# Three attention heads instead of two per exponential in a fused attention and feed-forward kernel

## The chip, the cores and the metric

One core of a Trainium2 chip runs the whole program. The metric is the device time of one execution in microseconds (us). The profile of an execution counts from its first to its last instruction and is about 1.8 us shorter than that time.

## The reference, cut to what matters

```python
# x is 1 x 2048 x 640 bf16; 32 query heads of 20 columns, one key head, one value head; F = 1536
xn  = layernorm(x)
q   = (xn @ wq) split in 32 heads;  k = xn @ wk;  v = xn @ wv
p   = softmax(q k^T / sqrt(20))          # 32 x 2048 x 2048 exponentials
att = concat(p v) @ wo
ffn = relu(xn @ w1 + b1)**2 @ w2 + b2
out = x + att + ffn
```

The exponentials are the bulk: 32 x 2048 x 2048 numbers, on 128 lanes 1,048,576 columns.

## The kernel before

Queries are taken in 4 chunks of 512 (`QC`), heads in 8 groups of 4 (`G`), keys in 16 tiles of 128 (`KT`). A *block* is one chunk and one group, a *step* is one key tile of a block. In a step TensorE computes the transposed scores of four heads (one bank of PSUM each, the memory `ps` of eight banks of 512 float32 columns that the matmuls write to; the four matmuls side by side on four row strips), ScalarE takes two heads per ACTIVATE, and TensorE multiplies the exponentials with v (P·V) one step behind. The six score banks form a ring of three pairs. The two other banks are the P·V accumulator (`PVB`) and one spare bank (`MB`) for everything else: query projections (QT), the first feed-forward product (FFN), output projections (OUT). Those *units* are cut into groups of four 32-column matmuls that fill the steps. Filler matmuls with zero weights use up what remains, to keep TensorE's clock up.

```python
for j in range(NSTEP):                                  # 512 steps
    b, t = divmod(j, KT)
    for i in range(4):                                  # scores of four heads
        n = 2 * j + i // 2; p = n % 3
        ...   # i == 0 waits for the exponential 2j-2
        matmul(ps[:, 2 * p + i % 2, :], kT[32*i:32*i+DH, tile t], qT[32*i:32*i+DH, ...])
    for a in range(2):                                  # two exponentials of two heads each
        n = 2 * j + a; p = n % 3
        activation(out=PT[:, n % NSLOT, :, :], in_=ps[:, 2*p:2*p+2, :], func=Exp, ...)   # 128x1024
    # (cut) choose the groups of other work and the number of fillers from a time budget
    if j >= 1:
        emit_pv(j - 1, nfill)     # waits for both exponentials of step j-1; at t == 0 also for the
                                  # transpose that empties the accumulator; at t == KT-1 emits
                                  # transpose, reciprocal, multiply, transpose on VectorE
    # (cut) the groups of the unit in hand
```

The softmax here doesn't subtract the row's maximum and nothing guards it: scores larger than these inputs give would overflow.

## Time and profile before

| | us |
|---|---|
| time, median of 15 runs | 977.7 (977.0 to 978.7) |
| profile: prologue, to the start of the first exponential | 25.77 |
| profile: loop, first exponential's start to last one's end | 940.77 |
| profile: tail, to the last instruction | 9.10 |

The profile page of the kernel before: the span, busy times (us, share of the span, instructions), the granted TensorE clock (the share of its full clock that TensorE was allowed) in tenths over 40 slices, the chain that ended last by engine, and its two costliest groups (busy us, mean ns of one, idle time before them and what ended it):

```profile
span 975.6 us, 28817 instructions
...
PE 831.6 (85%) x13373; PEld 316.5 (32%) x13375; DVE 178.8 (18%) x321; ACT 961.6 (99%) x1072; POOL 62.4 (6%) x69
...
PEclk9999999999999999999999999999999999999998
...
ACT 98%; PE 1%; DMA 0%; DVE 0%; ACTq 0%; issue 0%; SPq 0%; DVEq 0%
...
L852 ACT ACTIVATE PT<-ps 128x1024 bf16<-128x1024 f32 x1024 | 940.7, 1107 | 0.6 <-PE ps L843 0.5
L781 PE MATMUL ps<-kT,zeros 128*32 128x512 bf16 x4720 | 315.5, 382 | 0.0
```

ScalarE is the bound, by its exponentials. The chain in order of time (start us, us, what):

```profile
38.78 547.43 ACT PT L852 x596
586.23 379.39 ACT PT L852 x413
```

### The profile page before, as it was taken

The numbers are of one execution on the slowest core, as the hardware profiler recorded it, in microseconds if no ns is written. First come the engines' busy times: TensorE is split into PE (matmuls) and PEld (weight loads), VectorE is DVE, ScalarE is ACT, GpSimd is POOL, SyncE is SP. The second block draws the span as 40 slices with busy tenths as digits, with TensorE's granted clock in tenths as the row PEclk, the third lists the DMA queues.
The fourth block names the chain that finished last, engine by engine and source line by source line (L and its number), as shares of the span: only waits on it lengthen the run. The fifth ranks groups of instructions, "written<-read, shape, count | busy, mean of one in ns | idle before, by whom it ended". The sixth has DMA issues, their size and how long they took to land.

```text
span 975.6 us, 28817 instructions
## 1 busy us (share of the span) xinstructions
PE 831.6 (85%) x13373; PEld 316.5 (32%) x13375; DVE 178.8 (18%) x321; ACT 961.6 (99%) x1072; POOL 62.4 (6%) x69
## 2 busy tenths in 40 slices
PE   7888888888888888888888888888888888888886
PEld 3323223222233333333333333333333333333332
DVE  7221100111111211101111111211202221201123
ACT  8999999999999999999999999999999999999996
POOL 3110000000000000000000000000001001100000
PEclk9999999999999999999999999999999999999998
DMA  9100000000000000000000000000000000000000
GB/s 306 36 1 2 2 2 1 2 2 1 2 2 9 2 8 2 2 8 2 9 2 1 9 2 9 2 9 2 2 9 2 8 2 2 8 2 9 2 9 28
DMA packets 9432, 12.70 MB, mean 13 GB/s; under 512 B 1761, under 2 KB 8674, under 8 KB 9314
## 3 DMA queue, kind: packets, MB, share of 16 engines
q1 hardware_dynamic: 8002, 10.82, 3.4%
q8 instruction: 105, 1.72, 0.7%
q10 hardware_dynamic: 1312, 0.05, 0.1%
q14 instruction: 13, 0.11, 0.0%
HBM read 8.25 MB, written 2.62 MB: 11 GB/s over the span
## 4 chain that ended last, share of the span: by engine, by line
ACT 98%; PE 1%; DMA 0%; DVE 0%; ACTq 0%; issue 0%; SPq 0%; DVEq 0%
ACT PT L852 96%; DMA x_sb<-in_A_x_dram 0%; ACT PT L434 0%; ACT OTn L434 0%; PE ps L221 0%; ACT PT L429 0%; ACT xnT L476 0%; ACT OTn L429 0%; DVE out_sb L357 0%; PE ps L497 0%; PE ps L407 0%; ACTq L84 0%; PE ps L815 0%; ACT vtmp L439 0%; PE ps L843 0%
## 5 line engine op out<-in xcount | busy, mean ns | idle before, releaser
L852 ACT ACTIVATE PT<-ps 128x1024 bf16<-128x1024 f32 x1024 | 940.7, 1107 | 0.6 <-PE ps L843 0.5
L781 PE MATMUL ps<-kT,zeros 128*32 128x512 bf16 x4720 | 315.5, 382 | 0.0
L815 PE MATMUL ps<-PT,vx 128*32 128x512 bf16 x2048 | 201.5, 384 | 74.4 <-ACT PT L852 74.1
L843 PE MATMUL ps<-qT,kT 20*128 20x512 bf16 x2048 | 201.9, 384 | 55.8 <-ACT PT L852 53.3
L781 PEld LDWEIGHTS ps<-kT,zeros 128*32 128x32 bf16 x4720 | 97.9, 95 | 127.9 <-issue 68.7
L843 PEld LDWEIGHTS ps<-qT,kT 20*128 20x128 bf16 x2048 | 51.4, 91 | 269.1 <-ACT PT L852 259.5
L815 PEld LDWEIGHTS ps<-PT,vx 128*32 128x32 bf16 x2048 | 53.7, 95 | 177.2 <-ACT PT L852 148.3
L790 DVE STREAM_TRANSPOSE Tn<-ps 128x512 f32<-128x512 f32 x32 | 23.0, 717 | 416.4 <-PE ps L815 416.4
L269 POOL TENSOR_TENSOR big<-hT_tmp 128x512 bf16<-128x512 bf16 x48 | 49.9, 1040 | 761.0 <-DVE hT_tmp L264 761.0
L221 PE MATMUL ps<-xnT,w_sb 128*32 128x512 bf16 x960 | 68.7, 380 | 0.0
L221 PE MATMUL ps<-w_sb,big 128*32 128x320 bf16 x1536 | 63.6, 300 | 0.0
L264 DVE TENSOR_SCALAR hT_tmp<-ps,b1col 128x512 bf16<-128x512 f32 x48 | 36.0, 750 | 144.0 <-PE ps L221 144.0
L221 PE MATMUL ps<-wo_pad,OTn 128*32 128x320 bf16 x1024 | 47.1, 304 | 2.6 <-DVE OTn L798 2.6
L221 PEld LDWEIGHTS ps<-w_sb,big 128*32 128x32 bf16 x1536 | 40.6, 96 | 15.7 <-issue 6.4
L221 PE MATMUL ps<-xnT,wq_sb 128*20 128x512 bf16 x640 | 45.5, 379 | 0.0
L320 DVE TENSOR_TENSOR out_sb<-ps,x_sb 128x320 bf16<-128x320 f32 x24 | 11.8, 492 | 149.1 <-PE ps L221 149.1
L221 PEld LDWEIGHTS ps<-wo_pad,OTn 128*32 128x32 bf16 x1024 | 27.9, 98 | 14.1 <-DVE OTn L798 2.9
L221 PEld LDWEIGHTS ps<-xnT,w_sb 128*32 128x32 bf16 x960 | 24.1, 96 | 19.5 <-issue 1.7
L246 DVE CAST qT<-ps 128x512 bf16<-128x512 f32 x32 | 22.1, 691 | 10.4 <-PE ps L221 10.4
L798 DVE STREAM_TRANSPOSE OTn<-T 128x512 bf16<-128x512 bf16 x32 | 22.8, 711 | 1.1
L792 DVE TENSOR_TENSOR T<-Tn 128x512 bf16<-128x512 f32 x32 | 22.2, 692 | 1.1
L221 PEld LDWEIGHTS ps<-xnT,wq_sb 128*20 128x20 bf16 x640 | 15.0, 90 | 13.2 <-issue 0.3
(70 smaller groups left out, 129.1 us busy)
## 6 DMA issues: line engine op xcount, KB each, us to landing
w_sb<-in_B_w_dram SPq DMA_DIRECT2D x2, 1920.0 KB, 10.5
out_dram<-out_sb SPq DMA_DIRECT2D x16, 160.0 KB, 1.8
x_sb<-in_A_x_dram SPq DMA_DIRECT2D x3, 640.0 KB, 7.3
wq_sb<-in_A_wq_dram SPq DMA_DIRECT2D x1, 800.0 KB, 10.2
wo_pad<-in_A_wo_dram SPq DMA_DIRECT2D x4, 200.0 KB
x_sb<-in_A_x_dram SPq DMA_DIRECT2D x2, 320.0 KB, 3.6
wk_c<-in_A_wk_dram ACTq DMA_DIRECT2D x1, 25.0 KB, 3.3
wv_c<-in_A_wv_dram ACTq DMA_DIRECT2D x1, 25.0 KB, 5.0
```

The costliest lines, as they stand in the source:

```text
L221: add(P.pe, lambda e, j=j, Lj=Lj, R=R, k=k, last=last, n=u.n, bank=bank, m=m: e.matmul(ps[32 * j:32 * j + m, bank, 0:n], Lj, R, start=(k = ...
L246: add(P.dve, lambda e: e.tensor_copy(out=qT[:, qc % 2, g, :], in_=ps[:, u.bank, :]), waits=w, inc=misc_free)
L264: v_relu = add(P.dve, lambda e: e.tensor_scalar(out=hT_tmp[:, k % 2, :], in0=ps[:, u.bank, :], scalar1=b1col[:, f:f + 1], scalar2=0.0, op0 ...
L269: add(P.pool, lambda e: e.tensor_tensor(out=h2T[:, qc % 2, f, :], in0=hT_tmp[:, k % 2, :], in1=hT_tmp[:, k % 2, :], op=ALU.mult), waits=w2 ...
L320: v = add(P.dve, lambda e: e.tensor_tensor(out=out_sb[:, slot, cs], in0=ps[:, u.bank, 0:320], in1=x_sb[:, st, cs], op=ALU.add), waits=w, i ...
L781: add(P.pe, lambda e, jj=jj: e.matmul(ps[32 * jj:32 * jj + 32, PVB, :], zeros32[:, :], kT[:, 0:512], start=False, stop=False, tile_positio ...
L790: add(P.dve, lambda e: e.transpose(out=Tn[:, a, :], in_=ps[:, PVB, :]), waits=w, inc=pv_evac)
L792: v2 = add(P.dve, lambda e: e.tensor_tensor(out=T2[:, a, :].rearrange("p (c d) -> p c d", d=32), in0=Tn[:, a, :].rearrange("p (c d) -> p c ...
L798: add(P.dve, lambda e: e.transpose(out=OTn[:, qc % 2, g, :], in_=T2[:, a, :]), waits=w3, inc=norm_done)
L815: add(P.pe, lambda e, i=i, n=n, t=t: e.matmul(ps[32 * i:32 * i + 32, PVB, :], vx[:, t, :], PT[:, n % NSLOT, i % 2, :], start=(t == 0), sto ...
L843: add(P.pe, lambda e, i=i, p=p, t=t, qc=qc, g=g: e.matmul(ps[:, 2 * p + i % 2, :], kT[32 * i:32 * i + DH, t * 128:(t + 1) * 128], qT[32 * ...
L852: add(P.act, lambda e, n=n, p=p: e.activation(out=PT[:, n % NSLOT, :, :], in_=ps[:, 2 * p:2 * p + 2, :], func=AF.Exp, bias=-EXP_SHIFT, sca ...
```

## The change

Its intent: the columns of the exponentials stay the same, but fewer instructions carry them, so their fixed cost is paid less often. Three heads fill three PSUM banks, 1536 columns; two sets of three banks use the same six banks. The 32 heads become ten groups of three and one of two (the *two-head block*, sixth of the eleven blocks of a chunk). Steps go from 512 to 704. P·V runs two steps behind, three at the start of a block. The four VectorE instructions of the normalisation are spread over steps. The budgets for units and fillers are cut to the shorter step.

```diff
-ST, DT, FT, G, QC, KT = 16, 5, 12, 8, 4, 16
-NSLOT = 8
+ST, DT, FT, QC, KT = 16, 5, 12, 4, 16
+HPG = 3
+G = (H + HPG - 1) // HPG
+NSLOT = 6
+NQS = 4
+GORDER = [0, 1, 2, 3, 4, G - 1, 5, 6, 7, 8, 9]
-    misc_budget_ns=900.0,
-    fill_target_ns=1500.0,
+    misc_budget_ns=620.0,
+    fill_target_ns=1060.0,
+    short_fill=1,
 (cut: query buffers, weights and units regrouped by three heads; T2 zeroed; normalisation deferred)
+            step_ns = 1344.0 if nh == HPG else 918.0
+            sset = 3 * (j % 2)
-            for i in range(4):
+            for i in range(HPG):
-                    if j >= 1:
-                        w.append((act_done, 2 * j - 1))
+                    if j >= 2:
+                        w.append((act_done, j - 1))
-            for a in range(2):
-                (two activations of 1024 columns)
+            add(P.act, lambda e, ...: e.activation(out=PT[:, j % NSLOT, 0:nh, :], in_=ps[:, sset:sset + nh, :], func=AF.Exp, ...),
+                waits=[(st_done, j + 1)], inc=act_done)
+            pvs = []
+            for k in (j - 3, j - 2):
+                first_of_block = (k % KT == 0 and k >= KT)
+                if (k == j - 2 and not first_of_block) or (k == j - 3 and first_of_block):
+                    pvs.append(k)
-            if CFG["enable_fill"] and j >= 1:
-                while busy + COL_NS <= CFG["fill_target_ns"] + COL_NS / 2:
+            if CFG["enable_fill"] and pvs:
+                while busy + COL_NS <= CFG["fill_target_ns"] - (1344.0 - step_ns) + COL_NS / 2:
                     nfill += 1
+                if nh < HPG and nfill == 0 and ngroups == 0:
+                    nfill = CFG["short_fill"]
```

## The prediction

> **What bounds the kernel now.** ScalarE. The page gives ACT 961.6 of 975.6 us, and the chain of waits that ended last is 96% the exponential of the scores: 1024 ACTIVATEs of 128x1024, from 25.8 to 966.5 us. Of the 975.6 us, 25.8 are prologue, 940.8 the exponentials, 9.1 the tail (last P·V, normalisation, last projection, output). TensorE is 85% busy, but part of that is filler matmuls that keep its clock up (4720 of them, granted clock 1.00).
>
> **What one exponential costs.** In the timeline, start to start of neighbouring exponentials is 904 ns where nothing delays them; the 128x640 evictions of the prologue are 584.5 ns apart. Two sizes give 0.833 ns a column plus 51 ns fixed (853.3+51, 533.3+51). The Trainium skill, "ScalarE: Activation LUTs", section "What ACT_TABLE_LOAD costs", states 0.833 ns a column and 186 less about 93 ns of overlap: the slope agrees, the fixed part is smaller here. The ACT lane is called 100% busy, but not all pitches are 904: summed, they hold 14.2 us more, and most sits at fixed places of each 16-step block. The second step's exponential comes about 200 ns late (mean 1101), others 20 to 80. The cause in the timeline: TensorE stands in the first P·V of a block until VectorE's 0.72 us transpose frees the accumulator, and a score matmul has only one 0.9 us exponential to hide behind.
>
> **What the change does.** Three heads per exponential instead of two, two PSUM sets of three banks, P·V two steps behind (three at a block start), the normalisation spread over steps. Columns stay the same (per chunk and key tile 10x1536+1x1024 = 16384). Instructions fall from 1024 to 640 of 1536 and 64 of 1024.
> - Fixed cost: 320 fewer x 51 ns = 16.4 us removed. Floor: 640x1331 + 64x904 = 909.7 us, against 926.1 before.
> - Gaps: a score matmul now has a whole exponential (1.33 us) to be late in, and P·V no longer waits at block starts. I expect 12 of the 14.2 us to go.
> - TensorE gets more steps (704 for 512), so more score and P·V groups. From start-to-start times in the timeline: scores 324 ns, a 4-column group of 512 216, of 320 135, the switch back to scores 106. A step with three 512-groups of other work: 324+216+648+106 = 1294 of 1331 ns; with four 320-groups 1186; the two P·V at a block's fourth step reach 1.5 us, which the slack absorbs; a two-head step with one filler 862 of 904. It fits, narrowly. Waits for the one spare bank can make TensorE late by some 0.3 to 0.6 us after query and FFN units, under the slack of about 0.8 us.
> - More query units (44 for 32) and projection groups on TensorE and VectorE, a larger weight memset on GpSimd: off the path. Prologue and tail: unchanged within 0.5 us.
>
> **Time.** 977.5 - 16.4 - 12 = 949 us. Range 946.2 to 954. Chances: faster by over 2% 0.93, within 2% 0.05, slower 0.02.
>
> **What would show the steps right or wrong.** Timeline: pitch of 1331 ns for three heads, 904 for two. By-form groups: 640 and 64 exponentials, about 912 us from first to last. Granted clock still 1.00. TensorE busy share about as before (80 to 90%), with fewer fillers. No 200 ns lateness at the block starts.
>
> **What would make it wrong.** A fixed cost that grows when an access spans three banks; TensorE falling behind in two-head blocks or after spare-bank waits, so gaps return (then nearer 954); the clock dropping with fewer fillers, which would make TensorE the limit and the kernel much slower.

## The result, and the profile after

| | before | after |
|---|---|---|
| time, median (us) | 977.7, 15 runs | 960.59, 11 runs (958.71 to 969.89) |
| ratio | | 0.9845 (0.982 to 0.9871) |
| profiled run: prologue | 25.77 | 27.22 |
| profiled run: loop | 940.77 | 928.88 |
| profiled run: tail | 9.10 | 10.90 |

A ratio is the mean time of one kernel's runs over that of the other's of the same rounds, so not quite the ratio of the medians. The change is 1.5% faster: outside the predicted range, and within the 2% that count as the same. The runs also spread: seven lie between 958.7 and 961.1 us, one at 963.1, and three near 969. The three slow ones have a mean granted clock of 0.980 or 0.981; the seven have 0.990 to 0.994. The profiled run is one of the slow ones (968.7 us), so the table above shows that case, not the median one.

The page of the changed kernel, the same lines, and its exponentials kept apart by shape:

```profile
span 967.0 us, 26310 instructions
...
PE 861.7 (89%) x12185; PEld 287.4 (30%) x12186; DVE 205.3 (21%) x381; ACT 941.0 (97%) x751; POOL 65.5 (7%) x71
...
PEclk9999999999999999999999998699999999999998
...
ACT 92%; PE 6%; DVE 1%; issue 1%; DMA 0%; ACTq 0%; SPq 0%; DVEq 0%
```

```profile
L891 ACT ACTIVATE PT<-ps 128x1536 bf16<-128x1536 f32 x640 | 861.9, 1809 | 3.0 <-PE ps L888 2.9
L891 ACT ACTIVATE PT<-ps 128x1024 bf16<-128x1024 f32 x64 | 61.8, 1213 | 6.2 <-PE ps L888 6.2
```

Three things differ from the expected picture. A three-head exponential takes 861.9 us / 640 = 1347 ns, not 1331. PEclk has a hole near 600 us. And TensorE, which had 1% of the chain, has 6%. The chain in order of time shows where:

```profile
156.82 439.80 ACT PT L891 x333
596.66 0.61 PE ps L888 x3
597.27 0.55 PE ps L859 x4
599.22 0.55 PE ps L814 x4
600.73 0.55 PE ps L814 x4
...
622.89 331.87 ACT PT L891 x252
```

For 440 us the chain is ScalarE alone. From 596.7 to 622 us it is TensorE, at steps of 1.51 us; then ScalarE alone again. The stretch is the third chunk's two-head block and the start of the next. The trace's clock record gives half clock from 596.60 to 620.50 us.

### What the starts hid

The prediction took the cost of an exponential from the spacing of its *starts*, 904 ns. Six neighbours of the kernel before, as the trace has them (us, duration in ns):

```
start     duration   end
81.667    1292       82.959
82.572    1305       83.877
83.476    1317       84.793
84.380    1330       85.710
85.299    1327       86.626
86.488    1055       87.543
```

The starts are 904 ns apart, then 919, then 1189: that last was the "200 ns late" start that the prediction called a gap. The ends are 918, 916, 917, 916, 917 ns apart, right through it. The recorded start runs ahead of the work by 12.5 ns per instruction, the interval grows by as much, and now and then a late score matmul takes the lead away again without delaying any end. Counted by ends, the loop before holds 1.7 us over 1024 x 917 ns, not 14.2. There was next to no gap to recover.

The Trainium skill, "Perfetto Trace Analysis", section "DVE / Act Engine Instruction", says what the two stamps are: the start is when the instruction begins in the ALUs, the end when its writes have been acknowledged. The trace fits that an end means finished work; the page does not say that the starts can lead by a growing amount.

### The profile page after: what moved, and what is told of

Same layout as the page of the kernel before. It is cut to its first block, busy times and chain, and to the rows that moved or that the text cites. A ratio compares the mean times of both kernels' runs of the same rounds, so it can differ in the third digit from the quotient of the medians.

```text
span 967.0 us, 26310 instructions
## 1 busy us (share of the span) xinstructions
PE 861.7 (89%) x12185; PEld 287.4 (30%) x12186; DVE 205.3 (21%) x381; ACT 941.0 (97%) x751; POOL 65.5 (7%) x71
## 3 DMA queue, kind: packets, MB, share of 16 engines
HBM read 8.25 MB, written 2.62 MB: 11 GB/s over the span
## 4 chain that ended last, share of the span: by engine, by line
ACT 92%; PE 6%; DVE 1%; issue 1%; DMA 0%; ACTq 0%; SPq 0%; DVEq 0%
ACT PT L891 91%; PE ps L888 2%; PE ps L859 1%; PE ps L814 1%; PE ps L242 1%; DMA x_sb<-in_A_x_dram 0%; PE ps L521 0%; ACT PT L453 0%; DVE qT L267 0%; DVE out_sb L379 0%; ACT OTn L458 0%; ACT PT L458 0%; PE ps L492 0%; ACTq L102 0%; PE ps L529 0%
## 5 line engine op out<-in xcount | busy, mean ns | idle before, releaser
L891 ACT ACTIVATE PT<-ps 128x1536 bf16<-128x1536 f32 (+1 forms) x704 | 920.6, 1755 | 9.2 <-PE ps L888 9.1
L888 PE MATMUL ps<-qT,kT 20*128 20x512 bf16 x2112 | 278.6, 389 | 66.4 <-ACT PT L891 59.8
L859 PE MATMUL ps<-PT,vx 128*32 128x512 bf16 x2816 | 274.8, 390 | 1.2 <-ACT PT L891 1.2
L814 PE MATMUL ps<-kT,zeros 128*32 128x512 bf16 x2316 | 186.6, 390 | 0.0
L888 PEld LDWEIGHTS ps<-qT,kT 20*128 20x128 bf16 x2112 | 68.5, 91 | 368.0 <-ACT PT L891 343.7
L859 PEld LDWEIGHTS ps<-PT,vx 128*32 128x32 bf16 x2816 | 70.6, 95 | 108.9 <-issue 77.2
L242 PE MATMUL ps<-wo_pad,OTn 128*32 128x320 bf16 x1408 | 65.9, 304 | 2.6 <-DVE part L365 2.6
L242 PE MATMUL ps<-xnT,wq_sb 128*20 128x512 bf16 x640 | 63.7, 387 | 1.8 <-DVE qT L267 1.8
L814 PEld LDWEIGHTS ps<-kT,zeros 128*32 128x32 bf16 x2316 | 37.7, 94 | 74.1 <-issue 74.1
L831 DVE TENSOR_TENSOR T<-Tn 96x512 bf16<-96x512 f32 (+1 forms) x44 | 30.3, 688 | 1.5
```

Source lines behind the costliest of these rows:

```text
L242: add(P.pe, lambda e, j=j, Lj=Lj, R=R, k=k, last=last, n=u.n, bank=bank, m=m: e.matmul(ps[32 * j:32 * j + m, bank, 0:n], Lj, R, start=(k = ...
L814: add(P.pe, lambda e, jj=jj: e.matmul(ps[32 * jj:32 * jj + 32, PVB, :], zeros32[:, :], kT[:, 0:512], start=False, stop=False, tile_positio ...
L831: st8["v2"] = add(P.dve, lambda e: e.tensor_tensor(out=T2[0:pp, a, :].rearrange("p (c d) -> p c d", d=32), in0=Tn[0:pp, a, :].rearrange("p ...
L859: add(P.pe, lambda e, i=i, t=t, hs=hs: e.matmul(ps[32 * i:32 * i + 32, PVB, :], vx[:, t, :], PT[:, j % NSLOT, hs, :], start=(t == 0), stop ...
L888: add(P.pe, lambda e, i=i, t=t, b=b, sset=sset: e.matmul(ps[:, sset + i, :], kT[32 * i:32 * i + DH, t * 128:(t + 1) * 128], qT[32 * i:32 * ...
L891: add(P.act, lambda e, j=j, nh=nh, sset=sset: e.activation(out=PT[:, j % NSLOT, 0:nh, :], in_=ps[:, sset:sset + nh, :], func=AF.Exp, bias= ...
```

## The experiments

Apart from the first, all computed a correct result. Experiments on the changed kernel share a fixed order in the prologue (see the second). "Loop" is from the first exponential's start to the last one's end in the profiled run.

### Exponentials alone

A program with nothing but exponentials from PSUM, in five phases: 40 of 1024 columns into separate memory without any semaphore, then 200 of 1024, 200 of 1536, 200 of 512 and 100 of 2048, each with a semaphore update and a long-satisfied wait.

> A wrong result on purpose: exponentials from PSUM alone, nothing else running, 40 of 128x1024 without semaphores, then 200 of 1024, 200 of 1536, 200 of 512, 100 of 2048 columns with one semaphore update and one long-satisfied wait each. Theory A (an exponential costs what its completions show: 64 ns + 0.833 ns a column, and the starts in the timeline only run ahead): end-to-end spacing 917, 1344, 490, 1770 ns for the four sizes, and the first-to-last time of each phase is that spacing times the count, whatever the starts say. Theory B (51 ns fixed, as the starts show, and the rest of the lateness before the change was gaps made by other engines): with no other engine, 904, 1331, 478, 1758 ns.

The groups by form (the 1024-column line holds both phases of that size):

```profile
L40 ACT ACTIVATE PT<-ps 128x1536 bf16<-128x1536 f32 x200 | 268.8, 2758 | 0.0
L40 ACT ACTIVATE PT<-ps 128x1024 bf16<-128x1024 f32 x240 | 220.2, 2154 | 3.2 <-DVE ps L27 3.2
L40 ACT ACTIVATE PT<-ps 128x2048 bf16<-128x2048 f32 x100 | 177.1, 2519 | 0.0
L40 ACT ACTIVATE PT<-ps 128x512 bf16<-128x512 f32 x200 | 98.1, 1884 | 0.0
```

Busy over count is 1344, 918, 1771 and 491 ns (in the order of the lines): theory A. By ends the spacings are 1343.3, 916.7, 1770.0 and 490.0, so 63.3 ns fixed plus 0.8333 ns a column. The starts in the same phases are 1330, 903.4, 1756.8 and 478.4 ns apart, with no other engine at work and no gap. Over 200 exponentials of 1024 columns the lead grew until one lasted 3659 ns on record; in the 512-column phase it stopped growing at 2905. The phase without semaphores showed the same two spacings (916.6 and 903.8), so the semaphores are not the cause. The lead is a property of the record; why it arises stays open.

### The change, with a fixed prologue order

The prologue's tasks are placed by a small list scheduler, written in the kernel, that walks a Python `set` of strings. The order of such a set differs from build to build. Built with three hash seeds, each of the two kernels came out with three different orders of prologue instructions.

```diff
-            unsched = set(tasks.keys())
+            unsched = dict.fromkeys(tasks)
```

> The changed kernel, with the prologue's task scheduler walking its tasks in a fixed order instead of a set's (the order of a set of strings differs from build to build). The loop is untouched: from first exponential start to last exponential end 919 to 920 us where the clock does not drop, and some runs of granted clock near 0.98 about 10 us longer, as in the changed kernel. If the 1.4 us longer prologue came from the change itself it stays at 27.2 us; if from the build's order, it moves, to 25 to 27 us.

959.76 us median of 5 (957.61 to 963.96), ratio 0.9821 (0.9797 to 0.9846). The first exponential of the profiled run starts at 28.79 us, outside what was expected, and the loop is 922.95 with two drops of the clock in it. So the prologue moved, but not to a better place. Two things go with its length. One is the build's order. The other is the clock: this run had half clock from 12.96 to 19.79 and from 23.20 to 26.61 us. Two later experiments have the same prologue, instruction for instruction: one started its first exponential at 26.56 us (half clock for 3.4 us), the other at 28.87 (10.2 us of it). So the same program moves by 2.3 us, and these runs do not show that the 1.4 us come from the change; the kernel before with a fixed order, in the next experiment, started its first exponential at 26.86 us.

### Two heads, with the later P·V alone

One part of the change in the kernel before (with the fixed prologue order there too): the first P·V of a block one step later, so that TensorE never stands before the transpose.

```diff
-            if j >= 1:
-                emit_pv(j - 1, nfill)
+            for k in (j - 2, j - 1):            # k >= 0
+                first_of_block = (k % KT == 0 and k >= KT)
+                if (k == j - 1 and not first_of_block) or (k == j - 2 and first_of_block):
+                    pvs.append(k)
+            (fillers as before; emit_pv for each of pvs)
```

> The kernel before (two heads, fixed prologue order), with one part of the change alone: the first P.V of a block one step later, so that TensorE no longer stands waiting for the transpose there. Theory A: the exponentials still end 917 ns apart, loop 939.5 to 940.8 us, at most 1.5 us won. Theory B, of the prediction: the late starts at the second step of the blocks were gaps, so some 6 us or more are won, loop 935 us or less. In both, the 200 ns late starts at block starts should go or shrink.

978.13 us, ratio 0.9999 (0.9987 to 1.0012); loop 940.28 against 940.77. The group of the exponentials:

```profile
L852 ACT ACTIVATE PT<-ps 128x1024 bf16<-128x1024 f32 x1024 | 940.1, 1118 | 0.8 <-PE ps L843 0.7
```

The 6 us were not there to win. One expectation common to both theories missed: the late start at the block's second step did not shrink (mean spacing 1109 ns, before 1101). So the prediction's cause for it, the wait for the transpose, was wrong as well. A block start in the timeline of the kernel before shows what stands there (lines of other instructions left out):

```profile
113.33 0.39 PE L843 MATMUL ps<-qT,kT 20*128 20x512 bf16 x4 [0.25 <-ACT PT L852]
...
114.25 0.40 PE L815 MATMUL ps<-PT,vx 128*32 128x512 bf16 x4 [0.52 <-ACT PT L852]
...
114.47 1.04 PE L221 MATMUL ps<-xnT,wq_sb 128*20 128x512 bf16 x16
114.70 0.72 DVE L790 STREAM_TRANSPOSE Tn<-ps 128x512 f32<-128x512 f32 x1 [18.86 <-PE ps L815]
...
115.45 0.40 PE L843 MATMUL ps<-qT,kT 20*128 20x512 bf16 x4
...
116.08 0.40 PE L815 MATMUL ps<-PT,vx 128*32 128x512 bf16 x4 [0.24 <-ACT PT L852]
```

The scores of the second step (115.45) follow, without a wait, the last P·V of the old block and 16 matmuls of the query projection. The P·V that needs the transpose comes only after them (116.08), so it cannot have made them late. The exponential of these scores starts at 115.89, just after they end, and 1180 ns after the start before it; the ends of the two are 916 ns apart. That the query projection makes these scores late is read from this order and was not tested.

### Every exponential as two instructions

The fixed cost doubled, in the changed kernel itself (with the edit of the section after the next, which keeps the clock up): two heads and one, or one and one, over the same columns.

```diff
-            activation(PT[:, j % NSLOT, 0:nh, :] <- ps[:, sset:sset + nh, :])
+            for h0, h1 in ((0, nh - 1), (nh - 1, nh)):
+                activation(PT[:, j % NSLOT, h0:h1, :] <- ps[:, sset + h0:sset + h1, :])
             (counts of act_done doubled)
```

> The fill-by-pace version with every exponential issued as two instructions (two heads and one, or one and one) over the same columns: 704 more instructions, all else equal. Theory A: 64 ns more a step, loop 918.5 + 704 x 0.0637 = 963.3 us plus what clock drops add. Theory B (51 ns and gaps): 954 us or less. If the number of exponentials did not matter: 919.

1002.17 us, ratio 1.0252 (1.0237 to 1.0267); loop 963.39 us, where theory A said 963.3.

```profile
L892 ACT ACTIVATE PT<-ps 128x512 bf16<-128x512 f32 x768 | 898.8, 1250 | 0.0
L892 ACT ACTIVATE PT<-ps 128x1024 bf16<-128x1024 f32 x640 | 895.3, 1728 | 0.8 <-PE ps L888 0.7
```

(The busy time of the two groups overlaps in time, so they don't add up; that too is the lead of the starts.) Against 918.97 us with 704 exponentials (below), 704 more cost 44.4 us, 63.1 ns each; the medians of the two versions' times differ by 44.3 us, without any profile. So the fixed cost measured alone and in place is the same. The loops of the two kernels fit it: 940.77 - 918.97 = 21.8 us for 320 instructions fewer, of which 320 x 63.3 ns are 20.3; the rest is the little that the loop before had beyond its exponentials (1.7 us) less what is left of it.

### No filler in the two-head blocks

```diff
-    short_fill=1,
+    short_fill=0,
```

> The changed kernel with fixed prologue order and no filler matmul in the two-head blocks. Theory C (the clock drops where TensorE has too little to do in the two-head blocks): clock drops in most or all runs, in more than one of the four two-head blocks, mean clock 0.98 or lower, and time 965 to 1000 us. Rival D (the drops are chance, unrelated to the fillers there): as many drops as in the run with one filler, about one run in four.

978.88 us in the median of 5, ratio 1.0006 (0.9992 to 1.0019): the whole gain gone, in every run alike (977.88 to 979.84), mean clock 0.949 to 0.958. Its granted clock over the 40 slices:

```profile
PEclk8999988999999995999999998699999999689999
```

After the prologue's dent there are four holes for four two-head blocks: half clock for 17.1, 23.9, 23.9 and 23.9 us by the clock record. Theory C holds, and chance is out: taking the one filler out of those steps turned a drop in some runs into drops in all.

The lengths of these stretches are multiples of 3.413 us (5 and 7 of them), and from one stretch's start to the next are 68, 69 and 69 of them. The Trainium skill, "TensorE: Matmul & The Clock Gate", section "What's actually happening", describes free-running windows of 3413 ns after which the clock is set to half or full; this agrees in the length and in the two levels.

### Where the drop comes from

In the profiled run of the changed kernel, the three windows around the drop (stretch, length, busy us and instructions of PE, PEld, DVE, ACT, POOL, then clock, DMA share, GB/s), and TensorE's timeline in the middle one:

```profile
589.78:593.19 3.41, 3.03 (x45) 0.87 (x42) 0.00 (x0) 3.41 (x4) 0.09 (x1) 1.00 0.00 0
593.19:596.60 3.41, 2.35 (x29) 0.53 (x25) 0.75 (x2) 3.41 (x5) 0.00 (x0) 1.00 0.02 5
596.60:600.02 3.42, 3.36 (x26) 0.66 (x26) 1.62 (x3) 2.59 (x4) 0.00 (x0) 0.50 0.00 0
```

```profile
592.46 0.62 PE L814 MATMUL ps<-kT,zeros 128*32 128x512 bf16 x8
592.90 0.39 PE L859 MATMUL ps<-PT,vx 128*32 128x512 bf16 x4
593.48 0.39 PE L888 MATMUL ps<-qT,kT 20*128 20x512 bf16 x3 [0.19 <-ACT PT L891]
593.80 0.40 PE L814 MATMUL ps<-kT,zeros 128*32 128x512 bf16 x4
...
594.83 0.39 PE L888 MATMUL ps<-qT,kT 20*128 20x512 bf16 x3 [0.41 <-ACT PT L891]
595.15 0.40 PE L814 MATMUL ps<-kT,zeros 128*32 128x512 bf16 x4
595.37 0.39 PE L859 MATMUL ps<-PT,vx 128*32 128x512 bf16 x4
595.74 0.39 PE L888 MATMUL ps<-qT,kT 20*128 20x512 bf16 x3
596.66 0.61 PE L888 MATMUL ps<-qT,kT 20*128 20x512 bf16 x3 [0.53 <-ACT PT L891]
```

At 592.46 a step has eight filler matmuls, at 593.80 and 595.15 four: these belong to the two-head block. But the score matmuls run two steps ahead of the exponentials, so those two steps are still 1.34 us apart (593.48 to 594.83), the pace of three heads. They have the work of a 0.92 us step in 1.34 us. The step at 595.74 has scores alone, since the first P·V is put off. That window has 2.35 us of TensorE work, the one before it 3.03. At half clock the two-head step needs 1.51 us for what ScalarE would take 0.92 us over, and it stays there until the block ends, although TensorE then hardly idles (3.36 of 3.42 us).

The remedy is to budget a step by the exponential that runs beside it, two steps earlier:

```diff
-            step_ns = 1344.0 if nh == HPG else 918.0
+            step_ns = 1344.0 if NH(BLK(max(j - 2, 0) // KT)[2]) == HPG else 918.0
-                if nh < HPG and nfill == 0 and ngroups == 0:
+                if step_ns < 1344.0 and nfill == 0 and ngroups == 0:
```

> The changed kernel (fixed prologue order); the amount of TensorE work of a step is now set by the pace of the exponential that runs beside it, two steps earlier, instead of by the step's own heads: the first two steps of a two-head block keep the two fillers of the 1344 ns pace, the first two steps after it get the work of the 917 ns pace. Theory C: the stretch that dropped the clock was those two steps, still paced at 1344 ns but filled for 917; so no drop in or beside the two-head blocks in the profile, and the times of the runs lie within 1.5 us of each other apart from prologue drops, loop 918.5 to 920 us. Rival D (chance): one run in three still has a drop in the loop.

957.85 us in the median of 4 (957.35 to 962.13), ratio 0.9804 (0.9789 to 0.9819); loop 918.97 us, no drop in it. The exponentials by form, the chain's longest piece, and the window in which the same block begins:

```profile
L891 ACT ACTIVATE PT<-ps 128x1536 bf16<-128x1536 f32 x640 | 861.7, 1881 | 0.9 <-PE ps L888 0.8
L891 ACT ACTIVATE PT<-ps 128x1024 bf16<-128x1024 f32 x64 | 60.5, 1238 | 0.0
```

```profile
29.68 914.51 ACT PT L891 x701
```

```profile
594.54:597.96 3.42, 3.06 (x44) 0.73 (x32) 2.37 (x4) 3.42 (x5) 0.00 (x0) 1.00 0.02 5
```

From the fourth exponential to the last the chain is one piece of ScalarE; ScalarE waited for scores 0.9 us in all, against 9.2 in the changed kernel. Three of the runs agree within 0.6 us; the fourth (962.13, clock 0.986) is slower, and as no profile was taken of it, where its clock fell is not known. So the expectation that all runs agree was not quite met. The other profiles decide against chance. The six of versions with this edit (this run, the moved left-over units, the three of the section after, and the exponentials in two) have 24 two-head blocks and no drop at any. The three without it and with one filler (the changed kernel, its fixed order, five groups) have 12 and three drops; the one without filler has 4 and four drops. By run times, four of 23 runs with one filler and without the edit lie at 968.7 us or more; of the 22 runs with it, those of the split exponentials aside, none lies above 962.2.

How little work is too little remains open. In the two-head blocks the emptiest window of each is telling: without filler it has at most 2.41 us of TensorE work and all four dropped; in the changed kernel it has 2.62, 2.48, 2.35 and 2.61 us, and only the 2.35 dropped; with fixed order 2.49 dropped and 2.48 did not; in the fill-by-pace run none is under 2.80 and none dropped. So where the windows happen to lie over the thin steps goes with whether a run drops. But busy time is not the measure everywhere: the kernel before has windows of 2.40 us (81.46 to 84.87), and its later P·V one of 2.05 (55.97 to 59.38), that no drop followed, while in the first block a drop followed 2.77 us (fixed order, 30.02 to 33.44).

### The tail

The prediction had the tail unchanged; it is 1.8 us longer. The timeline before, then of the changed kernel, from the last transpose of the normalisation:

```profile
968.81 0.71 DVE L798 STREAM_TRANSPOSE OTn<-T 128x512 bf16<-128x512 bf16 x1
969.57 1.74 PEld L221 LDWEIGHTS ps<-wo_pad,OTn 128*32 128x32 bf16 x32 [2.88 <-DVE OTn L798]
```

```profile
958.36 0.71 DVE L839 STREAM_TRANSPOSE OTn<-T 128x512 bf16<-128x512 bf16 x1
959.00 0.45 DVE L365 TENSOR_TENSOR part<-ps,part 128x320 f32<-128x320 f32 x1
959.57 2.57 PEld L242 LDWEIGHTS ps<-wo_pad,OTn 128*32 128x32 bf16 x44 [2.94 <-DVE OTn L839]
...
960.64 0.49 DVE L365 TENSOR_TENSOR part<-ps,part 128x320 f32<-128x320 f32 x1 [1.19 <-PE ps L242]
```

Before, 32 matmuls follow (eight last projections of four). After, there are 44: three groups of a left-over partial projection come first, and its eviction (L365) stands before the eight last ones on VectorE. The partial projections had been spread over too few groups a step to be done in time. Five groups a step instead of four:

```diff
-    misc_budget_ns=620.0,
+    misc_budget_ns=700.0,
```

> The changed kernel (fixed prologue order), budget for other matmul work in a step 620 to 700 ns, so that a projection unit takes five groups a step instead of four and no partial projection is left over after the last exponential. If those left-over units made the tail 10.9 instead of 9.1 us, the tail comes back to 9.0 to 9.3 us; if the tail grew from the spread-out normalisation, it stays at 10.5 to 10.9. Loop as before, with clock drops as in the changed kernel.

The tail is 9.09 us: the left-over units were the cause, not the spread-out normalisation. (The same tail took 10.47 us in the run with the fixed order, so about 0.4 of the 1.8 us differs from run to run.) The time was not better for it (964.8 us, median of 6, ratio 0.9863 with an interval of 0.9837 to 0.989). The profiled loop, 925.35 us, has clock drops in the first block and in a two-head block, and besides about a dozen exponentials that end some 150 to 200 ns late. The fill-by-pace run, with four groups, has none of these after the first 5 us of its loop; that five groups leave TensorE no slack is the likely reason, not tested by itself.

A second way failed. The left-over units were issued before the last P·V, on top of the fill by pace, where TensorE waits for the last exponential anyhow.

```diff
+        (left-over units moved up to here)
         emit_pv(NSTEP - 1, 0)
         (rest of the deferred normalisation)
-        (left-over units)
```

> The fill-by-pace version, with the left-over partial projections issued before the last P.V (while TensorE waits for the last exponential) instead of behind the last normalisation. Tail 10.1 to between 9.1 and 9.4 us, loop 919 us with no drop, time about 957 us in runs without a prologue drop of length; ratio to before about 0.979.

The tail stayed at 10.08 us. The units fit into the wait except for the eviction between the two of them, and the last P·V came as much later as the end came earlier. Time 958.81 us (median of 4), ratio 0.9804 (0.9789 to 0.9819).

### Towards a version that beats both

Fill by pace, five groups, and filler matmuls also in shorter gaps of the prologue's plan:

> Both edits (fill by pace, five groups) and more filler matmuls in the prologue's gaps. Prologue shorter than 28.8 us, loop 918.5 to 920, tail 9.0 to 9.3: span 953 to 957 us, time 955 to 959, with runs that agree within 2 us. If drops remain in the prologue, the first exponential starts at 27 to 29 us.

958.16 us, ratio 0.9797 (0.9785 to 0.981), four runs within 0.17 us. First exponential at 26.87 us, loop 920.5 (the late ends of the five groups), tail 9.10.

Fill by pace and the moved left-over units, with 27 instead of 22 warm-up matmuls at the start:

> The same with 27 instead of 22 warm-up matmuls at the start, to keep TensorE occupied until its first transposes. If the prologue's half-clock stretches follow from its idle TensorE windows, there are fewer of them and the first exponential starts up to 1 us earlier than 26.6; else no change beyond 0.3 us.

957.47 us, ratio 0.9794 (0.978 to 0.9809). In the profiled run the prologue had no stretch at half clock and the first exponential came at 25.35 us, the earliest of all. But the clock fell from 29.85 to 36.68 us, in the first block, and the loop was 921.3 us: what was won was given back.

Fill by pace, the warm-up, one more filler in steps of the first block, five groups in one block of the last chunk only:

> A version meant to beat both kernels: fill by pace, 27 warm-up matmuls, one more filler in the steps of the first block that have room, and five projection groups a step in one block of the last chunk only. First exponential at about 25.4 us, loop 919 to 920 us without drops, tail 9.1 us: span 953.5 to 955, time 955 to 957 us, ratio to before about 0.977. If the first block's drop (2.7 us in the run with more warm-up) comes back, 958.

957.36 us (956.13 to 957.73, 5 runs), ratio 0.9788 (0.9774 to 0.9801); profiled run 26.41 + 919.87 + 9.08 us. All its runs lie under the fastest run of either kernel (977.0 and 958.7), though not all in the same rounds. The prologue again had 3.4 us at half clock, so it is not the 25.4 us hoped for, and the time lies just above what was expected.

## Why the prediction was wrong, point by point

- **"51 ns fixed", so "16.4 us removed".** Mis-sized: the fixed cost is 63.3 ns (exponentials alone) and 63.1 ns (every exponential split). 320 fewer remove 20.3 us. The slope of 0.833 ns a column was right.
- **"I expect 12 of the 14.2 us to go."** This is the step that failed. The 14.2 us were taken from the spacing of starts. They were the 12.5 ns a piece, 12.8 us in all, by which starts lead, handed back at the places where the lead ended. By ends the loop had 1.7 us to spare. The cause given for them, P·V waiting for the transpose, did not make the starts late either: those P·V come after the late scores. The later P·V alone gave 0.5 us of loop and nothing in time.
- **"Floor: 640x1331 + 64x904 = 909.7 us."** It is 640 x 1343.3 + 64 x 916.7 = 918.4 us, and the version without drops ran in 918.97. The prediction's own loop, 940.8 - 28.4 = 912.4 us, lay under that floor: no run could have reached it. These two terms together are 6.6 us of the error.
- **"Prologue and tail: unchanged within 0.5 us."** The tail grew by 1.8 us, by left-over projections: a first partial projection now has 20 groups (13, and one for each of 7 head groups), before 17; the units were counted in the prediction's work but not placed step by step. The prologue was 1.4 us longer in the profiled run; that differs from build to build and run to run.
- **The clock.** Named as a danger ("the clock dropping with fewer fillers"), but as a matter of the whole kernel, at a small chance. It came at one place, in some runs: 23.9 us at half clock, of which the loop lost about 10 us (928.88 - 918.97).
- **The sum.** 949 + 6.6 (loop) + 1.8 (tail) + 1.4 (prologue) = 958.8 us, about where the runs without a long drop lie (958.7 to 961.1).
- **What was right.** ScalarE bounds both kernels; TensorE's step fits, from the 324, 216, 135 and 106 ns read before: at full clock ScalarE waited 0.9 us in 919. TensorE's busy share rose only from 85 to 89%, with fewer fillers. Three PSUM banks in one access cost nothing extra: the fixed part is the same for 512 to 2048 columns.

## What to carry to other kernels

Take the cost of a pipelined instruction from the spacing of its ends, or from busy time over count in a stretch without waits, not from starts as this trace has them: if the mean of one is longer than busy over count, the intervals overlap and late starts may be no gaps at all. On an engine that hardly waits, merging instructions saves the fixed cost times the number removed and no more, so compute that floor first and hold every claimed gain against it. Where one engine runs ahead of another by some steps, budget its work by the pace of the step it runs beside, and lay the units out step by step to the very end, since what is left over lands in the tail.

## What the Trainium skill lacked or had wrong

- "ScalarE: Activation LUTs", section "What ACT_TABLE_LOAD costs": 186 ns + 0.833 ns a column, less about 93 ns of overlap back to back, gives an estimate of 946 ns for 1024 columns; the section doesn't say from which memory. Measured back to back from PSUM: 916.7, so 63.3 ns fixed. The slope agrees. "Perfetto Trace Analysis", section "Optimizing Scalar/DVE Operations", does tell the memories apart: about 93 ns for ScalarE on SBUF and about 51 on PSUM. The starts here give 50.1 (903.4 less 853.3), the ends 63.3.
- "Perfetto Trace Analysis", section "DVE / Act Engine Instruction": nothing there says that the recorded starts of back-to-back ACTIVATEs lead the ends by a growing amount (starts 903.4 ns apart, ends 916.7; up to 3659 ns on record for an instruction that takes 917).
- "TensorE: Matmul & The Clock Gate", section "Why this matters for your kernels", asks for "No PE-idle gaps >~3µs between matmul bursts". Here the clock dropped after a window of 3.41 us in which TensorE was busy 2.35 us and no idle stretch of it exceeded 0.53 us; and it stayed at half through seven windows with 3.35 us or more busy. So that row alone is not enough. The same page, section "A second HAM failure mode: psum-queue depth-cycling", tells of drops from frequent short idle stretches, but the page gives no share of work that is enough, and these runs don't settle it either.
